# Sinkhorn-sorted attention and top-1 experts on one core: the units of attention in pairs, and the second half's sorting in a new order

## The chip, the cores and the metric

The kernel runs on one core of a Trainium2 chip. The metric is the device time of one execution in microseconds, the median of several; the kernel before took 172.33 us (three runs, 172.12 to 172.53).

The engines are named as in the rows of the profile: PE is TensorE (matmuls; PEld is its loading of weights), ACT is ScalarE, DVE is VectorE, POOL is GpSimd, SP is SyncE. Each works through its own list of instructions in order and waits for the others by semaphores. Matmul results land in PSUM, eight banks, from which ACT or DVE must fetch ("empty") them before the bank can be written again.

## The reference, cut to what matters

Four batches of eight heads, 768 rows in eight blocks of 96, 64 wide. A learned 8x8 matrix per head, made doubly stochastic in five rounds, mixes the blocks of K and of V; each block of Q attends to the mixed block of its number. The result, 3072 rows of 512, goes through eight experts of which each row uses the one with the largest gate:

```python
k_sorted = np.einsum('bhij,bhjcd->bhicd', P, k_b)          # mix the blocks of K, and of V
scores = scale * np.matmul(q_b, k_sb.transpose(0, 1, 2, 4, 3))
attn = np.exp(scores - max); attn = attn / (attn.sum() + 1e-09)
x = np.matmul(attn, v_sb)                                   # 3072 x 512 after the heads are joined
logits = x @ w_gate + modality_bias[modality_id]; e_idx = np.argmax(logits, axis=1)
out[mask] = gate_w[mask, None] * (np.maximum(x[mask] @ w1[e], 0.0) @ w2[e])   # for each expert e
```

The modality bias is so strong that all rows of one modality use one expert. The kernel counts on that (and has a slow path, not taken here): it has two experts, A and B, and sorts the rows by modality.

## The kernel before

**Attention.** The work is two halves of 16 units. Unit u takes four heads of two batches for one block: `scores` (eight small matmuls, tile `sc`), `expo` (one exponential of 96x768 on ACT into `attnT`), `av` (eight small matmuls, tile `op`; the 65th column is the sum of the weights), and on DVE a reciprocal (`rs_all`) and a multiplication into `xb`. Two units make one block of 96 rows for two batches. Before a half's units can run, V and K must be mixed: `sort_v` (eight chunks, tile `va`) and `sort_k` (six chunks, `ka`), and the queries turned, `prep_q` (tile `tq`). For the second half the V that was loaded into `v_in` is first copied in another order into `kv` by POOL (`relay_v`, four copies); K is then loaded into the place of V.

**Placement.** For each pair of units `place` multiplies `xb` by a permutation, so that rows of modality A stand from the left and rows of B from the right of `XT` (tile `pm`), and two casts of 72-wide windows bring them there at an offset that the engine first loads into a register (`load_offs`). `side` says which engine casts.

**Experts.** The rows are cut into 15 slots of 128 or 256 rows (the last of 224), each of A or of B, and each can start when so many blocks are placed. A slot has: `mG`, the gate's logits (tile `lg`) and their small steps on DVE and ACT; `mL1`, the first layer in two halves of 16 or 32 matmuls (tile `hp`), each half in two banks whose ReLU goes to `hT` by ACT or DVE; `mL2`, the second layer for 128 rows (tile `yp`), multiplied by the gate into `y` and scattered to the output by POOL. Which engine empties a bank was chosen by `pick`, from a running count of what each engine has been given.

**Order.** The program's order is each engine's order. `do_unit(u)` (from line 725) emits the scores of unit u+1, its exponential, one expert piece of the first list that can run (`run_pieces`), the output of unit u, and, where one is pending, a placement. So between two outputs there is always a unit's scores and one expert piece. In units 0 to 5 `av` also issues three or four matmuls of 252 columns into a spare part of its tile (line 474), whose results nobody reads; they are called fillers here. The tiles `sc`, `hp`, `op`, `pm` (of the blocks from 3 on), `va` and `ka` share three places of two banks each; `lg`, `tq`, `yp` (and `pm` before) share two places of one bank. A tile gets the place that was given up first, and its first matmul waits for the engine that empties the tile before it.

POOL also issues all large loads, in its order among its other work. After the units of the first half the kernel mixes V and K for the second with expert pieces between the chunks.

Of the kernel before, what the change touches and what calls it, by code (L numbers as in the profile page):

```python
# [24 lines left out]
def kernel(  # L25
# [442 lines left out]
    def av(u):  # L468
# [22 lines left out]
    def side(t, r):  # L491
        if t in (1, 7):
            return ("act", "dve")[r]
        return "act" if t % 2 == 0 or t == 5 else "dve"

    def load_offs(t):
        for o0, o1 in ([(0, 1), (1, 2)] if t in (1, 7) else [(0, 2)]):
# [54 lines left out]
    def mG(s):  # L552
# [11 lines left out]
        la, es, gt = la_all[:, ts], es_all[:, ts], gate[:, ts]  # L564
        nc.vector.tensor_tensor(la, lg[:, 0:nz, 0:E], bc_mid(st["bAB"][:, mi], nz), ALU.add)
        for z in range(nz):
# [3 lines left out]
            else:  # L570
                nc.vector.tensor_copy(dst, src)
        nc.scalar.activation(es, la, ACT.Exp)
# [5 lines left out]
    def relu(dst, src, n):  # L578
        if pick(n) == "act":
# [3 lines left out]
    def mL1(s, half):  # L583
# [4 lines left out]
        for b in range(2):  # L588
# [9 lines left out]
            ins = relu(hT[s % 2][:, half * 4 + b * nf // 2:half * 4 + (b + 1) * nf // 2, 0:n], hp[:, fs, 0:n], 512)  # L598
            tc.add_to_no_dep_group(grp, ins.ins)

    def mL2(s, z):
# [20 lines left out]
        else:  # L622
# [4 lines left out]
            if pick(512) == "act":  # L627
# [8 lines left out]

    pieces = []
    for s in range(NS):
        n = SLOTS[s][2]
        a = [(mG, (s,)), (mL1, (s, 0))]  # L640
        if s:
            a.append((mL2, (s - 1, 0)))
        if n > 128:
            a.append((mL1, (s, 1)))
        if s and SLOTS[s - 1][2] > 128:
            a.append((mL2, (s - 1, 1)))
        if s == 2:

            a = a[2:3] + a[:2] + a[3:]
        pieces += [(s, f, x) for f, x in a]  # L650
    pieces += [(NS - 1, mL2, (NS - 1, z)) for z in reversed(range(NZ[-1]))]
    pairs = [0]

    def can_run(piece):
        s, f, a = piece
        if f is mL2:
            return not any(p[1] is mL1 and p[2][0] == a[0] for p in pieces)
        return SLOTS[s][3] <= pairs[0] and not any(p[1] is mL2 and p[2][0] <= s - 2 for p in pieces)

    def run_pieces(n):  # L660
        ran = []
        while n:
            here = next((p for p in pieces if can_run(p)), None)
            if here is None:
                break
            pieces.remove(here)
            here[1](*here[2])
            ran.append(here)
            n -= 0 if here[1] is mG else 1
        return ran  # L670
# [45 lines left out]
    rank_off()  # L716
    for r in range(2):
        load_q(1, 0, r, 0)
    for z in range(2, 4):
        load_v(1, z)  # L720
    pending, ready = [], []

    def do_place():
        t = pending.pop(0)
        load_offs(t)
        place(t)
        ready.append(t + 1)

    def do_unit(u, last, n):
        if u < last:  # L730
            scores(u + 1)
            if u == 4:
                do_place()
            expo(u + 1)
            if u == 6:
                prep_q(0, 1, 2)
        if u == 13:

            for hq in range(2):
                prep_q(1, 0, hq, "dve")  # L740
        if 4 < u < 8:
            n = 0
        run_pieces(n)
        if ready:
            pairs[0] = ready.pop()
        av(u)
        if u in (4, 5, 7):
            prep_q(0, 1, u - 4)
        if u in (5, 7):
            run_pieces(1)  # L750
        if u % 2 == 0 and pending:
            do_place()
        if u % 2:
            pending.append(u // 2)

    for u in range(16):
        do_unit(u, 15 if u != 7 else 8, 2 if u == 12 else 1)
        if u == 8:
            make_bd(1)
        if u == 6:  # L760
            rank_p(1)
        for z in {9: (0, 1), 10: (2,), 11: (3,)}.get(u, ()):
            relay_v(z)
            if z:
                load_k(1, z - 1)
# [3 lines left out]
    for ch in range(8):  # L769
        sort_v(1, ch, ("act", "dve", "dve", "act")[ch] if ch < 4 else ("dve", "act")[ch % 2])  # L770
        if ch == 1:
            do_place()
        if ch in (1, 4):
            run_pieces(1)
        if ch == 3:
            pairs[0] = ready.pop()
    for ch in range(6):
        sort_k(1, ch, ("dve", "act")[ch % 2] if ch < 5 else "both")
        if ch in (1, 4):
            run_pieces(1)  # L780
    for hq in range(2, 4):
        prep_q(1, 0, hq)
    scores(16)
    expo(16)
    for u in range(16, 32):
        do_unit(u, 31, 1)
        if u in (16, 20):
            rank_p(u // 4 - 2)
        if 17 <= u < 21:
            prep_q(1, 1, u - 17)  # L790
    while ready or pending:
        run_pieces(1)
        if ready:
            pairs[0] = ready.pop()
# [229 lines left out]
```

## Time and profile before

| | |
|---|---|
| median of 3 runs | 172.33 us (172.12 to 172.53) |
| the profiled execution | 171.09 us |
| its span, first to last instruction | 169.4 us |
| PE busy | 150.5 us (89%) |
| DVE, ACT, POOL busy | 100.8 (60%), 94.9 (56%), 78.9 us (47%) |
| unit 0's output on PE | from 27.6 us of the span |
| unit 15's and unit 31's output | 65.7 and 127.8 us |
| last matmul | 164.2 us |

The profile shows one execution. Times in it are counted from the first instruction. The kernel has a start (to about 27 us: loads, the 8x8 matrices, mixing for the first half), the first 16 units (to 66), the mixing for the second half (to 83), the second 16 units (to 128) and experts alone (to 164); then the last rows are written. A busy PE is not PE at its peak, and ends of matmuls are modelled, so lengths of steps are best read from starts, or from the chain of waits.

### The profile page before, as it was taken

Reading aid. Unit: us, or ns where it says so; the run is one execution under the profiler, and the core shown is the slowest. Engines: PE = TensorE matmul, PEld = TensorE weight load, DVE = VectorE, ACT = ScalarE, POOL = GpSimd, SP = SyncE. Lnnn points to the kernel's source line nnn. Section 1 sums busy time; section 2 is a strip of 40 time slices with the busy share of each in tenths; the row PEclk is TensorE's granted clock in tenths of the full one; section 3 lists DMA queues with packets and bytes.
Section 4 is the critical chain, followed back from the end, with each engine's and each line's share of the span. In section 5 each row is a group of like instructions: output and inputs, shape, how many; then the busy total and the mean of one; then the engine's idle time right before and its main releaser. Section 6 shows DMA issues by size and latency. Waiting matters only on the chain.

```text
span 169.4 us, 5303 instructions
## 1 busy us (share of the span) xinstructions
PE 150.5 (89%) x2219; PEld 113.7 (67%) x2235; DVE 100.8 (60%) x261; ACT 94.9 (56%) x153; POOL 78.9 (47%) x150
## 2 busy tenths in 40 slices
PE   0489898899999999999899999999899999999970
PEld 0138886788667588777676768866677667776740
DVE  2778688578495387867675496674945613233430
ACT  4214767887557567665538757868466443432410
POOL 6888899778139997940204022020122222242432
PEclk9999999999999999999999999999999999999997
DMA  3999999999999988999101111001111111112221
GB/s 37 193 214 211 199 203 202 197 191 203 199 212 199 262 153 147 229 165 165 61 9 62 66 64 68 0 0 66 62 66 64 59 69 62 62 66 90 96 72 65
DMA packets 16303, 20.36 MB, mean 120 GB/s; under 512 B 9841, under 2 KB 11921, under 8 KB 16274
## 3 DMA queue, kind: packets, MB, share of 16 engines
q0 software_dynamic: 15648, 19.93, 60.5%
q8 instruction: 18, 0.29, 0.7%
q1 hardware_dynamic: 626, 0.05, 0.3%
q14 instruction: 11, 0.09, 0.2%
HBM read 27.31 MB, written 6.49 MB: 199 GB/s over the span
## 4 chain that ended last, share of the span: by engine, by line
PE 65%; POOL 9%; DVE 7%; issue 6%; ACT 6%; DMA 5%; POOLq 0%; ACTq 0%
PE hp L592 22%; PE yp L625 22%; DMA q_in<-in_q_dram 5%; PE sc L459 4%; PE op L479 4%; PE tq L334 3%; ACT XT L528 2%; PE pm L516 2%; POOL out_dram L631 2%; PE ka L324 2%; DVE xb L484 2%; PE va L311 2%; PE lg L560 2%; PE op L474 1%; POOL v_in L135 1%
## 5 line engine op out<-in xcount | busy, mean ns | idle before, releaser
L631 POOL DMA_INDIRECT out_dram<-y,ids x25 | 24.7, 989 | 77.8 <-ACT y L628 32.6
L625 PEld LDWEIGHTS <-hT 128*128 128x128 bf16 x192 | 17.6, 98 | 18.4
L465 ACT ACTIVATE attnT<-sc 96x768 bf16<-96x768 f32 x32 | 25.7, 807 | 6.7 <-PE sc L459 6.5
L580 ACT ACTIVATE hT<-hp 128x512 bf16<-128x512 f32 (+1 forms) x35 | 20.2, 588 | 11.6 <-PE hp L592 8.7
L592 PE MATMUL hp<-XT,wB 128*128 128x256 bf16 (+2 forms) x224 | 24.5, 263 | 0.2 <-DVE xb L484 0.2
L592 PE MATMUL hp<-XT,wA 128*128 128x128 bf16 (+1 forms) x256 | 23.1, 246 | 0.4 <-DVE xb L484 0.2
L484 DVE TENSOR_TENSOR xb<-op,rs_all 96x512 bf16<-96x512 f32 x32 | 22.0, 686 | 1.1
L625 PE MATMUL yp<-wA,hT 128*128 128x512 bf16 x88 | 21.5, 379 | 0.7 <-issue 0.5
L625 PE MATMUL yp<-wB,hT 128*128 128x512 bf16 x88 | 21.5, 379 | 0.6 <-issue 0.3
L592 PEld LDWEIGHTS <-wB 128*128 128x128 bf16 x224 | 19.8, 98 | 2.8 <-DVE xb L484 0.4
L628 ACT ACTIVATE y<-yp,gate 128x512 f32<-128x512 f32 x15 | 10.3, 688 | 19.1 <-PE yp L625 19.1
L592 PEld LDWEIGHTS <-wA 128*128 128x128 bf16 x256 | 19.3, 97 | 2.3 <-DVE xb L484 0.4
L528 ACT CAST XT<-pm 128x720 f32 x20 | 15.4, 768 | 4.5 <-PE pm L518 2.7
L581 DVE TENSOR_SCALAR hT<-hp 128x512 bf16<-128x512 f32 x15 | 10.3, 688 | 8.9 <-PE hp L592 8.8
L630 DVE TENSOR_SCALAR y<-yp,gate 128x512 f32<-128x512 f32 x9 | 6.8, 751 | 14.7 <-PE yp L625 14.7
L479 PEld LDWEIGHTS <-attnT 96*128 96x128 bf16 x256 | 11.8, 97 | 3.3
L483 DVE RECIPROCAL rs_all<-op 96x8 f32<-96x8 f32 x32 | 6.4, 199 | 11.7 <-PE op L479 11.6
L479 PE MATMUL op<-v_sb,attnT 96*128 96x65 bf16 x256 | 13.2, 193 | 0.0
L459 PE MATMUL sc<-qT,kT 64*128 64x96 bf16 x256 | 11.4, 205 | 1.9 <-DVE qT L102 0.7
L528 DVE CAST XT<-pm 128x720 f32 x12 | 10.9, 909 | 2.5 <-POOL pen L394 1.3
L147 POOL DMA_DIRECT2D q_in<-in_q_dram x16 | 12.3, 797 | 0.0
L100 ACT CAST v_sb<-va 96x1024 bf16<-96x1024 f32 x9 | 8.9, 1009 | 5.6 <-PE va L311 5.5
(166 smaller groups left out, 222.3 us busy)
## 6 DMA issues: line engine op xcount, KB each, us to landing
v_in<-in_v_dram POOLq DMA_DIRECT2D x8, 384.0 KB, 10.8
q_in<-in_q_dram POOLq DMA_DIRECT2D x16, 192.0 KB, 8.3
wA<-in_moe_w_dram POOLq DMA_DIRECT2D x4, 512.0 KB, 10.3
wB<-in_moe_w_dram POOLq DMA_DIRECT2D x4, 512.0 KB, 7.6
kv<-in_k_dram POOLq DMA_DIRECT2D x3, 512.0 KB, 10.8
v_in<-in_k_dram POOLq DMA_DIRECT2D x3, 512.0 KB, 6.2
out_dram<-y,ids POOLq DMA_INDIRECT x25, 2.8
modI<-in_moe_modality_id_dram SPq DMA_DIRECT2D x1, 24.0 KB, 4.4
```

The source lines that it names most:

```text
L147: nc.gpsimd.dma_start(out=q_in[r][z][:, 4 * hh:4 * hh + 4], in_=q[2 * g + r, 4 * hh:4 * hh + 4, z * 4 * BLK:(z + 1) * 4 * BLK] .rearrange( ...
L459: nc.tensor.matmul(sc[:, r, j * BLK:(j + 1) * BLK].rearrange("p (t r) -> p t r", t=3), kT[rows, x0:x0 + 128], qT5[rows, i // 4, h, :, i % ...
L465: nc.scalar.activation(attnT[u % 2][:, 0:8 * BLK].rearrange("p (r f) -> p r f", r=2), sc_tiles.pop(u)[0:BLK, :, 0:4 * BLK], ACT.Exp, scale ...
L479: nc.tensor.matmul(op[:, r, j * (D + 1):(j + 1) * (D + 1)], attnT[u % 2][:, c0:c0 + 128], v_sb[0:BLK, r * 64 + (hh * 4 + j) * 8 + i, 0:D + ...
L484: nc.vector.tensor_tensor(xb[t % XB][:, :, hh * 256:(hh + 1) * 256].rearrange("p r (j d) -> p r j d", j=4), o4[:, :, :, 0:D], rs_all[:, u] ...
L528: ins = (nc.scalar.copy if side(t, r) == "act" else nc.vector.tensor_copy)(d, s_).ins
L580: return nc.scalar.activation(dst, src, ACT.Relu)
L581: return nc.vector.tensor_scalar(dst, src, 0.0, None, ALU.max)
L592: mm = nc.tensor.matmul(hp[:, f, 0:n], w1_t[m][:, c, fc * 128:(fc + 1) * 128], XT[:, c, row:row + n], start=(c == 0), stop=(c == 3))
L625: nc.tensor.matmul(yp, hT[s % 2][:, f, hs], w2_t[m][:, f], start=(f == 0), stop=(f == 7))
L628: nc.scalar.activation(y, yp, ACT.Copy, scale=g_)
L631: ins = nc.gpsimd.indirect_dma_start(out=out, out_offset=bass.IndirectOffsetOnAxis(ap=ids[0:w, k_:k_ + 1], axis=0), in_=y[0:w], in_offset= ...
```

## The change

From unit 8 on the units are taken in pairs. A function `pair(t, one, two)` emits both units' scores and exponentials, then `one()`, then both outputs, then `two()`. In the plain case (`steady`) `one` holds the logits and a half of a first layer of a slot and the placement of the pair before, and `two` the rest of the gate's steps, at times a query transpose, and a second layer. The pieces of the experts are no longer found by a rule but written out by hand. In a pair the first bank of a half layer is emptied by DVE and the second by ACT (`DA`), second layers and query transposes by DVE, and all casts of placements by ACT but for one of block 1. The gate's exponential, sum and reciprocal (`gate_end`) come behind the outputs.

Units 0 to 7 keep their old order in the main, with these differences: units 4 and 5 have no fillers; the last transpose of the first half's queries stands ahead of unit 7's output instead of behind it; units 8 and 9 have their scores together, and the first layer of slot 1 behind them.

For the second half the two last loads of V stand ahead of two query loads; all four relay copies, the three loads of K and six query loads follow the scatter of slot 1 without a break, and the mixing has a new order of chunks and expert pieces. All four transposes of block 0 to 3's queries and one second layer more stand in it. Behind unit 31 the order of the experts is as before.

```diff
-        if u < 6:
+        if u < 4:
             for r in (0, 1, 0, 1)[:3 + (u > 2)]:
 ...
     def side(t, r):
-        if t in (1, 7):
-            return ("act", "dve")[r]
-        return "act" if t % 2 == 0 or t == 5 else "dve"
+        return "dve" if t == 1 and r else "act"
 ...
-    for r in range(2):
-        load_q(1, 0, r, 0)
     for z in range(2, 4):
         load_v(1, z)
+    for r in range(2):
+        load_q(1, 0, r, 0)
 ...
+    mG(0)
+    mL1(0, 0)
+    sc(7)
+    prep_q(0, 1, 2)
+    av(6)
+    put(2)
+    rank_p(1)
+    prep_q(0, 1, 3, "dve")
+    av(7)
+    DA = ("dve", "act")
+    def pair(t, one, two):
+        sc(2 * t, 2 * t + 1)
+        one()
+        av(2 * t)
+        av(2 * t + 1)
+        two()
+    def hidden(s, half):
+        if half == 0:
+            mG(s, late=True)
+        mL1(s, half, DA)
+    def steady(t, s, half, q_=None, l2=None):
+        def one():
+            hidden(s, half)
+            put(t - 1)
+        def two():
+            if half == 0:
+                gate_end(s)
+            if q_:
+                prep_q(*q_, "dve")
+            mL2(*l2, "dve")
+        pair(t, one, two)
+    steady(4, 1, 0, None, (0, 0))
+    make_bd(1)
+    steady(5, 2, 0, None, (1, 0))
+    for z in range(4):
+        relay_v(z)
+    for z in range(3):
+        load_k(1, z)
     for z, hh in ((0, 1), (1, 0), (1, 1)):
         for r in range(2):
             load_q(1, z, r, hh)
+    steady(6, 2, 1, None, (2, 0))
+    steady(7, 3, 0, None, (2, 1))
+    mL1(3, 1, DA)
+    put(7)
+    sort_v(1, 0, "act")
+    sort_v(1, 1, "dve")
+    mG(4)
+    mL1(4, 0, ("act", "act"))
+    sort_v(1, 2, "dve")
 ...
+    pair(8, lambda: hidden(5, 0), after_8)
+    steady(9, 6, 0, (1, 1, 1), (5, 0))
+    pair(10, before_10, after_10)
+    pair(11, before_11, lambda: mL2(7, 0, "dve"))
+    rank_p(3)
+    steady(12, 8, 0, None, (7, 1))
+    steady(13, 8, 1, None, (8, 0))
+    steady(14, 9, 0, None, (8, 1))
+    steady(15, 9, 1, None, (9, 0))
```

On POOL, before, from the last loads of V for the second half to the query loads (`kv` is written by the relay copies, `in_k_dram` is K, L631 is the scatter of a second layer's rows):

```order
L135 DMA v_in<-in_v_dram 128x1536 x2
L631 DMA out_dram<-y_86,ids 3072x512
L631 DMA out_dram<-y_87,ids 3072x512
L143 COPY kv<-v_in 128x64x24 x2
L139 DMA v_in<-in_k_dram 128x2048
L143 COPY kv<-v_in 128x64x24
L139 DMA v_in<-in_k_dram 128x2048
L143 COPY kv<-v_in 128x64x24
L139 DMA v_in<-in_k_dram 128x2048
L631 DMA out_dram<-y_88,ids 3072x512
L631 DMA out_dram<-y_89,ids 3072x512
```

The same place on POOL now (L635 is the scatter):

```order
L147 DMA q_in_74<-in_q_dram 128x4x192
L635 DMA out_dram<-y_86,ids 3072x512
L635 DMA out_dram<-y_87,ids 3072x512
L143 COPY kv<-v_in 128x64x24 x4
L139 DMA v_in<-in_k_dram 128x2048 x3
L147 DMA q_in_72<-in_q_dram 128x4x192
```

The K loads no longer stand between the copies but behind all four; the scatter ahead of the copies is still that of slot 1's rows (`y_87`), and the next scatters stand behind the query loads.

On ACT, before, around units 24 to 27 (`sc24` to `sc27` are the scores, `hp8` the first layer of slot 8, `pm10` and `pm12` placements, `y0` a second layer's result):

```order
L528 COPY XT_82<-pm10_2415 128x5x2x72
L465 ACTIVATE attnT0_77<-sc24_2428 96x768
L580 ACTIVATE hT1_85<-hp7_1_2438 128x512
L465 ACTIVATE attnT1_78<-sc25_2468 96x768
L572 ACTIVATE es_all_94<-la_all_93 128x16
L580 ACTIVATE hT0_84<-hp8_0_2495 128x512 x2
L465 ACTIVATE attnT0_77<-sc26_2543 96x768
L628 ACTIVATE y0_86<-yp7_0_2553,gate_95 128x512
L465 ACTIVATE attnT1_78<-sc27_2577 96x768
L580 ACTIVATE hT0_84<-hp8_1_2587 128x512 x2
```

The same units on ACT now, from the scores of unit 24 to the first layer beside units 26 and 27:

```order
L465 ACTIVATE attnT0_77<-sc24_2461 96x768
L465 ACTIVATE attnT1_78<-sc25_2470 96x768
L584 ACTIVATE hT0_84<-hp8_0_2495 128x512
L497 TENSOR_LOAD off_723
L526 ISA
L526 COPY XT_82<-pm11_2519 128x5x2x72
L526 ISA
L526 COPY XT_82<-pm11_2519 128x5x2x72
L576 ACTIVATE es_all_94<-la_all_93 128x16
L465 ACTIVATE attnT0_77<-sc26_2570 96x768
L465 ACTIVATE attnT1_78<-sc27_2579 96x768
L584 ACTIVATE hT0_84<-hp8_1_2590 128x512
```

The two exponentials of a pair stand together; one ReLU of the half layer follows instead of two or none, then the load of an offset and both casts of each placement, and the gate's exponential behind them; the second layers have left ACT.

## Rows read from the trace of the kernel before

**Rows 1.** Stretches: start:end, length, busy us (instructions) of PE PEld DVE ACT POOL, clock, DMA, GB/s

```profile
27.00:37.00 10.00, 9.33 (x181) 7.84 (x181) 7.07 (x21) 8.43 (x12) 7.78 (x26) 1.00 1.37 200
37.00:64.00 27.00, 25.75 (x396) 19.33 (x396) 17.27 (x48) 17.04 (x28) 19.08 (x17) 1.00 1.12 201
64.00:83.00 19.00, 18.20 (x378) 14.93 (x379) 13.90 (x21) 11.93 (x17) 9.52 (x12) 1.00 0.95 154
83.00:131.00 48.00, 45.93 (x669) 35.06 (x670) 30.87 (x79) 32.42 (x52) 8.33 (x9) 1.00 0.14 50
```

**Rows 2.** Chain of waits in order of time: start us, us, what

```profile
34.69 0.54 PE op L474 x4
...
41.17 1.80 PE hp L592 x32
...
65.89 0.24 PE op L479 x8
66.13 1.05 PE va L311 x16
...
77.98 1.64 PE ka L324 x96
...
84.20 0.21 PE lg L560 x5
...
88.81 0.46 PE tq L334 x12
...
106.64 0.24 PE op L479 x8
106.89 0.28 PE sc L459 x8
107.16 0.34 PE lg L560 x10
107.50 1.76 PE hp L592 x16
...
128.00 0.24 PE op L479 x8
...
148.55 1.73 PE yp L625 x8
```

**Rows 3.** Timeline of PE, a placement and what follows: start us, us, what

```profile
91.46 0.33 PE L516 MATMUL pm<-perm,xb 96*128 96x96 bf16 x4
...
91.98 0.53 PE L334 MATMUL tq<-ident,q_in 128*64 128x128 bf16 x12
```

**Rows 4.** Timeline of DVE and ACT near unit 4 and placement 2

```profile
34.97 0.69 DVE L484 TENSOR_TENSOR xb<-op,rs_all 96x512 bf16<-96x512 f32 x1
...
39.27 1.57 ACT L528 CAST XT<-pm 128x720 f32 x2
```

**Rows 5.** Page, costliest groups, the exponentials: busy us, mean ns; idle before

```profile
L465 ACT ACTIVATE attnT<-sc 96x768 bf16<-96x768 f32 x32 | 25.7, 807 | 6.7 <-PE sc L459 6.5
```

**Rows 6.** Timeline of PE and ACT behind a half layer

```profile
109.11 0.41 PE L479 MATMUL op<-v_sb,attnT 96*128 96x65 bf16 x8
...
109.31 0.60 ACT L580 ACTIVATE hT<-hp 128x512 bf16<-128x512 f32 x1 [0.28 <-PE hp L592]
```

**Rows 7.** Instructions of line 499, the offset loads on ACT: ns min/median/max

```profile
L499 ACTq TENSOR_LOAD <-off x11: 293/494/843, 29.6 to 125.7; - x11
```

**Rows 8.** Timeline of POOL, relays and a scatter, and ACT before it

```profile
51.70 5.67 POOL L143 COPY kv<-v_in 128x1536 bf16<-128x1536 bf16 x2
...
73.27 0.69 ACT L628 ACTIVATE y<-yp,gate 128x512 f32<-128x512 f32 x1 [1.53 <-PE yp L625]
...
74.23 1.04 POOL L631 DMA_INDIRECT out_dram<-y,ids  x1 [1.33 <-ACT y L628]
```

**Rows 9.** Page, DMA issues: KB each, median us from issue to landing

```profile
kv<-in_k_dram POOLq DMA_DIRECT2D x3, 512.0 KB, 10.8
v_in<-in_k_dram POOLq DMA_DIRECT2D x3, 512.0 KB, 6.2
```

More of the change, by code (lines that the diff above doesn't have):

```diff
@@ L491, in side @@
     def side(t, r):
-        if t in (1, 7):
-            return ("act", "dve")[r]
-        return "act" if t % 2 == 0 or t == 5 else "dve"
+        return "dve" if t == 1 and r else "act"
     def load_offs(t):
-        for o0, o1 in ([(0, 1), (1, 2)] if t in (1, 7) else [(0, 2)]):
+        for o0, o1 in ([(0, 1), (1, 2)] if t == 1 else [(0, 2)]):
             eng = ActEng if side(t, o0) == "act" else DveEng
@@ L550, in tiles, with mG @@
         return [(row, w0)] + [(row + w0 + 128 * z, 128) for z in range((n - w0) // 128)]
-    def mG(s):
+    def mG(s, late=False):
         m, row, n = slot(s)
@@ L563, in mG @@
         ts = slice(TOFF[s], TOFF[s] + nz)
[L564 removed]
+        la = la_all[:, ts]
         nc.vector.tensor_tensor(la, lg[:, 0:nz, 0:E], bc_mid(st["bAB"][:, mi], nz), ALU.add)
@@ L571, in mG, with gate_end @@
                 nc.vector.tensor_copy(dst, src)
+        if not late:
+            gate_end(s)
+    def gate_end(s):
+        ts = slice(TOFF[s], TOFF[s] + NZ[s])
+        la, es, gt = la_all[:, ts], es_all[:, ts], gate[:, ts]
         nc.scalar.activation(es, la, ACT.Exp)
@@ L635, in mL2 @@
         tc.add_to_no_dep_group("out", ins.ins)
[L637 to L670, printed above, removed]
     rank_b()
@@ L716, with sc, put @@
     rank_off()
+    for z in range(2, 4):
+        load_v(1, z)
     for r in range(2):
         load_q(1, 0, r, 0)
[L719 to L724, printed above, removed]
+    def sc(*us):
+        for u in us:
+            scores(u)
+        for u in us:
+            expo(u)
+    def put(t):
         load_offs(t)
         place(t)
[L727 to L765, printed above, removed]
+    sc(1)
+    av(0)
+    sc(2)
+    av(1)
+    sc(3)
+    av(2)
+    put(0)
+    sc(4)
+    av(3)
+    scores(5)
+    put(1)
+    expo(5)
+    av(4)
+    prep_q(0, 1, 0)
+    sc(6)
+    av(5)
@@ L768, with after_8, before_10, after_10 @@
             load_q(1, z, r, hh)
[L769 to L794, printed above, removed]
-        if pending:
-            do_place()
+    steady(6, 2, 1, None, (2, 0))
[7 more added lines that the diff above has]
+    sort_v(1, 2, "dve")
+    sort_v(1, 3, "act")
+    sort_v(1, 4, "dve")
+    mL2(3, 0, "dve")
+    sort_v(1, 5, "act")
+    sort_v(1, 6, "dve")
+    sort_v(1, 7, "act")
+    sort_k(1, 0, "dve")
+    sort_k(1, 1, "act")
+    mL1(4, 1, DA)
+    sort_k(1, 2, "dve")
+    prep_q(1, 0, 0, "act")
+    mL2(3, 1, "dve")
+    sort_k(1, 3, "act")
+    sort_k(1, 4, "dve")
+    prep_q(1, 0, 1, "act")
+    prep_q(1, 0, 2, "dve")
+    sort_k(1, 5, "act")
+    prep_q(1, 0, 3, "dve")
+    mL2(4, 0, "dve")
+    def after_8():
+        gate_end(5)
+        rank_p(2)
+        prep_q(1, 1, 0, "dve")
+        mL2(4, 1, "dve")
+    def before_10():
+        put(9)
+        mL2(6, 0, "dve")
+    def after_10():
+        prep_q(1, 1, 2, "dve")
+        mG(7)
+        mL1(7, 0, DA)
+    def before_11():
+        prep_q(1, 1, 3, "dve")
+        hidden(7, 1)
+        put(10)
+    pair(8, lambda: hidden(5, 0), after_8)
[7 more added lines that the diff above has]
+    steady(15, 9, 1, None, (9, 0))
+    mG(10)
+    mL1(10, 0)
+    put(15)
+    mL2(9, 1)
+    mL1(10, 1)
     cm = small("cm", 4)
@@ L823 @@
     last = NS - 1
-    while pieces:
-        for here in run_pieces(1):
-            if here[0] == last and here[1] is mG:
-                flag_b()
-            if here[0] == last and here[1] is mL1 and here[2][1] == 1:
+    for s in range(11, NS):
+        mG(s)
+        if s == last:
+            flag_b()
+        mL1(s, 0)
+        mL2(s - 1, 0)
+        if SLOTS[s][2] > 128:
+            mL1(s, 1)
+            if s == last:
                 flag_c()
+        if SLOTS[s - 1][2] > 128:
+            mL2(s - 1, 1)
+    mL2(last, 1)
+    mL2(last, 0)
     order.close()
```

14 lines of the change are left out of this document (8 added, 6 removed).

## The prediction

> **What bounds the kernel now.** I first read the stretches of the span with the busy time of each engine. TensorE (PE in the rows) is busy 9.33 of 10.00 us, 25.75 of 27.00, 18.20 of 19.00 and 45.93 of 48.00, and its granted clock is 1.00 in all of them [rows 1]. No other engine comes near that (ScalarE's 8.43 of the first 10 is the most), so PE's own order sets the time, and what a new order of the same matmuls can give back is PE's idle time: 0.67 + 1.25 + 0.80 + 2.07 = 4.8 us from 27 to 131. Behind 131 the kernel runs experts alone, in the same order before and after but for which engine empties a bank.
>
> Next I read the chain of waits in order of time: here one row is the length of one step on PE, and the reader is to take the unit prices from it [rows 2]: an output (op, 8 matmuls) 0.24, scores of a unit (sc) 0.28, the gate's logits (lg, 10) 0.34, half of a first layer (hp, 16) 1.76, one second layer (yp) 1.73, a query transpose (tq) 0.46, a chunk of sorted V (va) 1.05 / 2 = 0.53, a chunk of sorted K (ka) 1.64 / 3 = 0.55. A placement (pm, ten matmuls) is not whole in one row; from its start at 91.46 to the next step at 91.98 it takes 0.52 [rows 3]. Check: from the output of unit 23 at 106.64 to that of unit 31 at 128.00 stand 8 op, 8 sc, 2 lg, 4 hp, 4 pm and 4 yp, 1.92 + 2.24 + 0.68 + 7.04 + 2.08 + 6.92 = 20.88 by the prices and 21.36 in the rows: waits make up 0.48, 0.06 a unit.
>
> With them I lay the new order out on PE from a point where both orders have done the same work, and compare at four such points. "Behind" is the new kernel's time less the old one's at the same work done.
>
> **Start of the pairs, units 4 to 9.** Two units lose their fillers, four matmuls each: 2 x 0.54 = 1.08 us of PE [rows 2]. Little of it arrives. The first half layer of slot 0 writes a bank that the output of unit 4 had, and VectorE empties that at 34.97 + 0.69 = 35.66 [rows 4]. The end of the last filler, 34.69 + 0.54, is followed by output, transpose and logits, 0.24 + 0.46 + about 0.2, and so by the half layer at some 36.1; it moves by 0.3 to 0.4 (I take 0.3), and the rest turns into a wait. What follows is new. The last transpose of the first half of the queries now stands ahead of unit 7's output. It needs a bank that the first cast of placement 2 frees. The two casts took 1.57 from 39.27 [rows 4]; moved by 0.3 the first ends at 39.8. Transpose 0.46, output 0.24 plus 0.1 for a switch to other weights, scores of unit 8 0.28: 40.9. The half layer of slot 1 needs the exponential of unit 8 (its bank), 0.81 on ScalarE [rows 5]: it starts at 40.9 + 0.15 + 0.81 = about 41.9. Unit 9's scores wait in this time for the copy of that transpose, behind a 768-wide compare on VectorE, and cost nothing more. The half layer ends at 43.7. Before, it ran 1.80 from 41.17, and unit 9's scores followed: 43.25 [rows 2]. Behind by 0.45.
>
> **A pair in the steady state.** scores 2 x 0.28, logits 0.34, half layer 1.76, placement 0.52, outputs 2 x 0.24, second layer 1.73: 5.39 us with logits, 5.05 without. The added wait is at the second output: its bank is that of the half layer, whose second half ScalarE empties. In a row of before that step started 0.20 after the matmuls had ended (109.31, the next output at 109.11) and took 0.60 [rows 6]: 0.80, against placement and first output, 0.76. With a release this is about 0.1 us of wait in each of ten pairs; 5.5 and 5.15. Queued behind it on PE are a second layer and the next scores; all wait with it. If the wait were nothing I would win 1.0 in ten pairs, and if ScalarE came late by a whole exponential I would lose 8. I take 0.1 since nothing else is queued on ScalarE then: its two exponentials have ended some 0.5 us before. The casts are now all on ScalarE, and each needs its offset read first, 0.29 to 0.84 us [rows 7]; 0.80 + 0.3 + 1.57 = 2.7 after the half layer they end, and the next unit that needs their bank comes 0.52 + 0.48 + 0.1 + 1.73 + 0.28 = 3.1 after it. So they stay hidden, by 0.4.
>
> Pairs 4 to 7: from 43.7, rest of pair 4 (placement, outputs, wait, second layer) 2.85, then some 0.3 for the small matmul of make_bd and for logits that now need the bank of the second layer just before them, 5.5, 5.15, 5.5: 63.0. Before: unit 15's output ends at 65.89 + 0.24 = 66.13, with a half layer (1.76) and two transposes (0.92) more done: 63.45 [rows 2]. Behind by -0.45, so this stage gives 0.9.
>
> **Sorting of the second half.** Half layer 1.76, placement 0.52: PE is at the first chunk of V at 65.3. That chunk needs all four relay copies on GpSimd. Before, they began at 51.70, and two took 5.67 [rows 8]; now all four stand behind the scatter of slot 1. Its second layer ends at 43.7 + 2.85 + 0.3 + 5.5 = 52.35, and VectorE empties it behind two outputs and a gate, by about 53.3. A scatter starts 0.3 after its y (73.27 + 0.69 to 74.23) and takes 1.0 [rows 8], then 2 x 5.67: 65.9. So PE waits 0.6 where it did not before. Then 8 chunks of V 4.2, logits 0.34, two half layers 3.52, three second layers 5.19, 6 chunks of K 3.3, four transposes 1.84, two scores 0.56 = 18.95, and some 0.5 of short waits where a chunk's bank is not yet empty: 85.4. Before: the logits of slot 5 start at 84.20 with one second layer less done, 85.93 [rows 2]. Behind by -0.5.
>
> **Pairs 8 to 15.** Pair 8 has no placement: 0.2 + 1.80 + 0.48 + 0.1 + 0.46 + 1.73 = 4.8. Pairs 9, 10 and 11 by the same prices, with a transpose each: 5.85, 5.95, 5.6. That is 107.6. Before: the output of unit 23 ends at 106.88, one score more and one second layer less: 108.33 [rows 2]. Behind by -0.7, so 0.2 is won. Pairs 12 to 15: 2 x 5.5 + 2 x 5.15 = 21.3; before, 106.64 to 128.00, 21.36 [rows 2]. Nothing.
>
> **Tail.** The same steps on PE; VectorE takes most of the emptying in slots 10 and 11 at first, in about three quarters of PE's time. Nothing.
>
> **Sum.** +0.45 - 0.9 - 0.05 - 0.2 + 0 = -0.7 us. My lay-out has only the waits that I looked for, while the old kernel's times have all of theirs: PE idles 2.07 us in its 16 units from 83 to 131, 0.13 a unit [rows 1], of which I gave the new ones 0.05. The difference on 24 units is 1.9 that may be missing at most; I put a quarter, 0.5, in, since the check above left 0.06 a unit. So -0.2 us on the profiled execution (171.09: span 169.4 and 1.7 around it). That execution lies 1.24 below the median of the runs, 172.33; I carry the difference over: 172.1. A measurement of this kernel can tell 0.2%, 0.34 us, from no change; so the forecast is no change to speak of, with an own range of 171.1 to 173.1.
>
> Of the clock the rows say that it stays at the full level, 2.4 GHz, through stretches in which PE idles 4 to 7% [rows 1]; the new waits are under 1 us each, so the sum has no term for it. The Trainium skill, "TensorE: Matmul & The Clock Gate", section "What's actually happening", speaks against the change here: the array gets only half of its clock after it was idle, and the full one after it was busy again, and the fillers that go are work for just that. By that rule the result could be the fourth rival.
>
> **Rivals.**
> First, faster: the two junctions are covered. If the first half layer of slot 1 does not wait for unit 8, and the relays end before PE comes (their scatter 0.6 us sooner), 0.45 + 0.6 = 1.05 is not paid: 171.0. For it: VectorE and ScalarE are busy 63 to 84% of the stretches that hold them [rows 1], so either may be free earlier than I have it. Against it: both waits are for single named instructions, not for a queue.
>
> Second, slower: the K loads come late. They were issued one by one between relays and landed after 6.2 us in the median; now three are issued in a row at 65.9 with six query loads behind them. The three of the first half, issued in a row at the start, took 10.8 [rows 9]. PE needs the first at about 65.9 + 8.4 (8 chunks 4.2, logits 0.34, half layer 1.76, second layer 1.73, waits 0.4) = 74.3, that is 8.4 after the issue. Up to there it is free; at 10.8 it costs 2.4, 174.5. Against it: the loads at the start had four V loads ahead of them, and here the queue is empty.
>
> Third, the pairs do not change what is waited for: PE is never idle for what pairs remove, gains and losses are all under 0.1 us: 172.3.
>
> Fourth, the clock falls to 1.2 GHz after the wait at the sort. Were it there for one pair's length of work, the 5.4 us of that would be paid twice: 177.5. No row shows a granted clock under 1.00 before 131.
>
> **How the numbers follow.** Forecast 0.50, faster 0.22, slower 0.22, third 0.05, clock 0.01. The forecast's own spread (1.0 us either side of -0.2) has 0.43 of it more than 0.34 us below the old time, 0.32 within that and 0.25 above: faster 0.21 + 0.22 = 0.43; same 0.16 + 0.05 = 0.21; slower 0.13 + 0.22 + 0.01 = 0.36. The range reaches down to 170.4 (the faster rival, and half of the ten waits of 0.1 gone) and up to 174.2 (nearly the slower one's middle); beyond lie the late loads' upper end, the clock, and a gain above 1.9 us.
>
> **What would show it.** Right: in the new trace PE idles less from 44 to 63; a wait of some 0.6 us stands ahead of the first chunk of V and is ended by GpSimd's relay copy; the second output of a pair stands about 0.1 us late behind ScalarE's hT; the last output lies within 1 us of 128. Wrong: K chunks that wait for a DMA; scores that wait for casts of a placement; an idle time of PE from 84 to 130 well under 1 us or above 3; a granted clock under 1 before the tail.

## The result: slower by 0.7%, and the profile after

The changed kernel takes 173.53 us in the median of 7 runs (172.60 to 174.15), the kernel before 172.21 beside it; the ratio is 1.0071 (95%: 1.0050 to 1.0093). Run once more in the last series it came out at 1.0110 (1.0091 to 1.0128). The forecast was no change to speak of, 172.1.

The profiled execution is the shortest of the seven, 172.6 with a span of 171.0, against 171.09 and 169.4 before: 1.6 more. By stretches (columns as in [rows 1]):

```profile
27.00:37.00 10.00, 8.91 (x182) 7.55 (x182) 7.25 (x22) 8.81 (x13) 7.80 (x26) 1.00 1.37 199
37.00:64.00 27.00, 25.64 (x384) 19.05 (x382) 18.34 (x49) 17.89 (x28) 16.76 (x15) 1.00 0.97 177
64.00:83.00 19.00, 17.32 (x347) 13.81 (x346) 11.19 (x16) 11.28 (x15) 11.34 (x14) 1.00 1.06 177
83.00:131.00 48.00, 45.59 (x682) 32.84 (x676) 31.69 (x80) 28.87 (x44) 8.68 (x9) 1.00 0.15 56
```

PE is idle 1.68 from 64 to 83 (0.80 before) and 2.41 from 83 to 131 (2.07), at a granted clock of 1.00 throughout. The reader is to see that the two bad stretches are those of the sorting and of pairs 8 to 15, not the one of the first pairs.

The chain of waits in order of time (start, us, what) shows the sorting stage, where [rows 2] had whole chunks in a row:

```profile
62.91 2.79 POOL kv L143
65.70 0.04 issue
65.74 1.07 PE va L311 x16
...
74.81 0.45 issue
75.27 0.28 PE ka L324 x6
...
81.46 0.75 DVE y L634
82.21 0.04 issue
82.25 0.53 PE tq L334 x12
82.78 0.33 PE ka L324 x13
83.11 0.67 issue
83.79 0.47 PE ka L324 x19
```

Four things stand ahead of PE here: the relay copy, which takes 2.79 (two took 5.67 in [rows 8]; PE idle 0.67 at 65.74), a stop inside a K chunk for which the profile shows no releaser (0.45), a transpose that waits for a second layer's evacuation (0.36 of PE), and a second stop inside a K chunk, after 13 of its 32 matmuls (0.67).

The same view for pairs 8 to 11:

```profile
91.24 0.94 DVE perm L420
92.17 0.48 DVE qT L102
92.65 0.04 issue
92.69 0.27 PE lg L558 x5
...
101.02 0.75 DVE y L634
...
103.44 0.46 DVE qT L102
...
104.64 0.60 DVE hT L585
105.28 0.04 issue
105.32 0.61 ACT hT L584
105.93 0.04 issue
105.97 1.91 PE hp L596 x16
```

Twice the chain runs through VectorE. The logits of slot 6 start 0.46 late, since their bank's transpose is copied behind a compare of 0.94. The second half layer of slot 7 starts 1.03 late: VectorE does an evacuation, two outputs, a copy and a gate from 101.02 on before it empties the first bank, and ScalarE's part of the same half layer waits for VectorE's.

And a pair that goes as laid out, pair 12:

```profile
110.69 0.45 PE sc L459 x16
111.14 0.34 PE lg L558 x10
111.48 1.76 PE hp L596 x16
...
113.67 0.24 PE op L479 x8
113.93 0.40 PE op L479 x8
114.33 1.73 PE yp L629 x8
116.06 0.45 PE sc L459 x16
```

From scores to scores 5.37; the second output stands 0.40 where an output takes 0.24, so 0.16 for ScalarE's half of the half layer, whose length was read from [rows 6].

At the four points of the prediction and at the end of pair 15 the new kernel is behind, at equal work, by +0.16 (placement at 43.41 for 43.25), -0.71 (62.74 for 63.45), +1.00 (86.93 for 85.93), +2.29 (110.62 for 108.33) and +1.68 (131.49 for 129.81). It had 0.24 less on the clock when the first changed instruction came (unit 5's scores at 31.35 for 31.59).

| stage | forecast | measured |
|---|---|---|
| start of the pairs | +0.45 | +0.40 |
| pairs 4 to 7 | -0.9 | -0.87 |
| sorting | -0.05 | +1.71 |
| pairs 8 to 11 | -0.2 | +1.29 |
| pairs 12 to 15 | 0 | -0.61 |
| tail | 0 | 0 |

### The profile page after: what moved, and what is told of

Same layout as the page of the kernel before. It is cut to its first block, busy times and chain, and to the rows that moved or that the text cites. A ratio compares the mean times of both kernels' runs of the same rounds, so it can differ in the third digit from the quotient of the medians.

```text
span 171.0 us, 5301 instructions
## 1 busy us (share of the span) xinstructions
PE 150.8 (88%) x2227; PEld 111.7 (65%) x2227; DVE 105.6 (62%) x273; ACT 89.2 (52%) x140; POOL 78.7 (46%) x150
## 3 DMA queue, kind: packets, MB, share of 16 engines
HBM read 27.31 MB, written 6.49 MB: 198 GB/s over the span
## 4 chain that ended last, share of the span: by engine, by line
PE 51%; POOL 18%; issue 11%; DVE 8%; DMA 5%; ACT 4%; POOLq 1%; ACTq 0%
PE hp L596 17%; PE yp L629 14%; POOL kv L143 7%; DMA q_in<-in_q_dram 5%; POOL out_dram L635 5%; PE op L479 4%; PE tq L334 3%; PE sc L459 3%; PE va L311 3%; PE ka L324 2%; DVE xb L484 2%; DVE y L634 2%; PE pm L514 2%; ACT XT L526 2%; PE lg L558 1%
## 5 line engine op out<-in xcount | busy, mean ns | idle before, releaser
L635 POOL DMA_INDIRECT out_dram<-y,ids x25 | 25.1, 1002 | 80.2 <-DVE y L634 43.3
L465 ACT ACTIVATE attnT<-sc 96x768 bf16<-96x768 f32 x32 | 24.5, 803 | 10.8 <-PE sc L459 10.8
L526 ACT CAST XT<-pm 128x720 f32 x31 | 23.9, 771 | 4.7 <-PE pm L516 1.7
L585 DVE TENSOR_SCALAR hT<-hp 128x512 bf16<-128x512 f32 (+1 forms) x26 | 17.6, 683 | 11.4 <-PE hp L596 11.0
L584 ACT ACTIVATE hT<-hp 128x512 bf16<-128x512 f32 (+1 forms) x24 | 14.2, 592 | 17.1 <-PE hp L596 15.1
L629 PE MATMUL yp<-wA,hT 128*128 128x512 bf16 x96 | 22.7, 379 | 0.0
L634 DVE TENSOR_SCALAR y<-yp,gate 128x512 f32<-128x512 f32 x20 | 15.0, 748 | 11.4 <-PE yp L629 11.3
L479 PEld LDWEIGHTS <-attnT 96*128 96x128 bf16 x256 | 10.2, 97 | 1.8 <-issue 0.2
L143 POOL COPY kv<-v_in 128x1536 bf16<-128x1536 bf16 x4 | 11.2, 2850 | 0.0
L102 DVE CAST v_sb<-va 96x1024 bf16<-96x1024 f32 x7 | 8.5, 1219 | 4.3 <-PE va L311 4.2
L576 ACT ACTIVATE es_all<-la_all 128x16 f32<-128x16 f32 (+1 forms) x15 | 3.2, 211 | 13.9 <-DVE la_all L563 13.9
```

The source lines that it names most:

```text
L143: nc.gpsimd.tensor_copy(kv[:, 0:BLK * D].rearrange("p (d c) -> p d c", c=BLK)[:, :, cs], v_in[:, cs].rearrange("p c d -> p d c"))
L465: nc.scalar.activation(attnT[u % 2][:, 0:8 * BLK].rearrange("p (r f) -> p r f", r=2), sc_tiles.pop(u)[0:BLK, :, 0:4 * BLK], ACT.Exp, scale ...
L479: nc.tensor.matmul(op[:, r, j * (D + 1):(j + 1) * (D + 1)], attnT[u % 2][:, c0:c0 + 128], v_sb[0:BLK, r * 64 + (hh * 4 + j) * 8 + i, 0:D + ...
L526: ins = (nc.scalar.copy if side(t, r) == "act" else nc.vector.tensor_copy)(d, s_).ins
L629: nc.tensor.matmul(yp, hT[s % 2][:, f, hs], w2_t[m][:, f], start=(f == 0), stop=(f == 7))
L634: nc.vector.tensor_scalar(y, yp, g_, None, ALU.mult)
```

## The experiments

Each is an edit of the changed kernel, unless said, shown with its loops written short; ratios are to the kernel before, run beside it. The changed kernel itself stands at 1.0071 and 1.0110. These two differ by 0.4% for one and the same kernel, so what a single edit is worth is read from its trace, and the ratio only bears it out.

**Relays between the loads (e1).**

```
+    relay_v(0), relay_v(1)                  # ahead of steady(5): slot 1's scatter comes behind
     steady(5, 2, 0, None, (1, 0))
-    for z in range(4): relay_v(z)
-    for z in range(3): load_k(1, z)
+    load_k(1, 0); relay_v(2); load_k(1, 1); relay_v(3); load_k(1, 2)
```

> Two relay copies move ahead of the scatter of slot 1 (GpSimd is free from 49.3), the three K loads stand between the later relays as in the kernel before, then the six query loads. Main theory: the changed kernel loses in the sorting stage by the relay wait (0.67) and by gaps inside K chunks (0.45 + 0.67) that come from the nine loads landing in one burst at 72 to 82. Here the first V chunk does not wait and the loads end some 4 us earlier, so both go at least in part: 0.7 to 1.8 us shorter than the changed kernel, 171.7 to 172.8. Rival (the gaps belong to the order of PE's own instructions, not to the loads): 0.67 less and the gaps stay at the same chunks, 172.9. Second rival (PE only waits later, for K): no gain, 173.5.

0.9972 (0.9960 to 0.9983). Both stops are gone, but the relay wait is still there, 0.61: the first relay had to wait for its V load until 51.82, and the scatter stood in the middle. So the gain is that of the K chunks and what queued behind them: from the first V chunk to the scores of unit 16 the stage took 18.76 for 20.74. The edit moves relays and K loads at once, so it does not say which of the two counts.

**Four query loads later (e2).**

```
-    for z, hh in ((0, 1), (1, 0), (1, 1)): load_q(1, z, r, hh)
+    load_q(1, 0, r, 1)                      # r in 0, 1; the other four behind sort_k(1, 2)
```

> Four of the six query loads (those of the last quarter of the queries) move 14 us later in GpSimd's queue; nothing else changes. Burst theory: the second gap in a K chunk (0.67) and the wait of 0.36 at a query transpose behind it go, the first gap (0.45, among the K loads) stays or shrinks: 0.6 to 1.0 us shorter than the changed kernel, 172.5 to 172.9; a new gap may show at 84 to 88 where the loads now land. Rival (the gaps follow PE's instructions): no change, both gaps stay. Second rival: the first transpose of pair 8 waits for its query load, up to 1 us longer.

1.0069 (1.0054 to 1.0084): nothing won. The stop is longer, after the same 13 matmuls. Its PE timeline (start, us, engine, line, what; in brackets the idle time ahead):

```profile
82.52 0.40 PE L324 MATMUL ka<-bd,v_in 64*64 64x64 bf16 x13
84.26 0.47 PE L324 MATMUL ka<-bd,v_in 64*64 64x64 bf16 x19 [1.34 <-issue]
```

This run does not test the burst. GpSimd runs ahead of PE in its list, so the four loads were not issued 14 us later but 6 to 7 (the third to sixth query load stand between 68.8 and 71.9 in the changed kernel):

```profile
75.04 1.62 POOL L147 DMA_DIRECT2D q_in<-in_q_dram  x2
```

They were under way when PE stopped: the DMA share is 1.52 from 80 to 81 and 1.63 from 81 to 82.

**The four query loads left out (e5).** Those units compute with the first half's queries.

```
-    for z, hh in ((0, 1), (1, 0), (1, 1)): load_q(1, z, r, hh)
+    load_q(1, 0, r, 1)
```

> The changed kernel without the four query loads of its last quarter (those units then use the first half's queries); every other instruction stands as it was. In four profiles the last K chunk stops after 13 matmuls, 0.67 to 1.34 us, at the same instruction, and PE goes on 1.1 to 1.45 us after a 16 KB packet of the instruction queue has been moved (81.3 to 82.6 in the changed kernel); with the relays between the loads that packet came at 79.3, the loads had ended, and there was no stop. Theory (PE's next instructions come late because loads hold the DMA engines): without the 0.77 MB that end at 83, the packet comes before 80 and the stop goes; with it the wait of 0.36 behind it may go: 0.7 to 1.1 us shorter than the changed kernel. Rival (it is the place in the program alone): the stop stays, 0.7 or more, no change.

The theory's number failed: the stop stays, 0.62. That does not clear the loads: those that are left run to about 80 (DMA share 0.99 from 79.0 to 79.5, 0.63 and 0.21 in the next two half microseconds), and the packet of the expectation comes at 80.17, when they let up. All work ends 1.47 earlier than in the changed kernel's profile (the last scatter starts at 165.32 for 166.79), and yet it takes 175.19 (1.0235; 1.0212 to 1.0259): 8.2 us of its span lie behind the start of that scatter, for 4.2 in the changed kernel, and no row of the engines stands there. What they are stays open; the runs don't tell.

**Fillers back in units 4 and 5 (e6).**

```
-        if u < 4:
+        if u < 6:
```

> The changed kernel with the four filler matmuls back in units 4 and 5 (2 x 0.54 us of PE). The prediction had 0.3 to 0.4 of these 1.08 arrive, the rest lying under waits for casts. In the changed kernel three waits for casts and outputs follow (0.45, 0.40, 0.18) up to the placement at 43.41. Theory: that placement starts 0.2 to 0.5 later, 0.2 to 0.5 longer in all. Rival (PE had the time to spare only by 0.45): 1.0 later.

1.0048 (1.0022 to 1.0073), so by the ratio the fillers cost nothing that can be seen. The half layer of slot 1 starts at 41.86 for 41.63: 0.23 later, as expected. This run told more than it was meant to. It has 8 matmuls more ahead of the K chunks, and the stop moved by 8:

```profile
82.67 0.63 PE L324 MATMUL ka<-bd,v_in 64*64 64x64 bf16 x27 [0.70 <-issue]
```

27 matmuls are left of the chunk instead of 19. The stop stands at a count of PE's instructions, not at a tile.

**Slot 7's gate late and its first half layer on ScalarE (e3), and each alone (e10, e11).**

```
-        mG(7); mL1(7, 0, DA)
+        mG(7, late=True); mL1(7, 0, ("act", "act"))     # e10: late alone; e11: ("act", "act") alone
...
         hidden(7, 1)
+        gate_end(7)                                      # not in e11
```

> In pair 10 and 11 slot 7's gate ends after its second half layer, and ScalarE empties both banks of its first half layer. Theory: the 1.03 wait ahead of that second half layer is VectorE's queue (a second layer's evacuation, two outputs, a transpose copy and a gate from 101.0 to 104.6 ahead of the first bank, and ScalarE's part waits for VectorE's). With both on ScalarE they end at 104.6 and the wait is under 0.15: 0.9 us shorter than the changed kernel, 172.6. Rival (it is the exponential of the gate that holds ScalarE): only what the gate took, 0.4, is won. Second rival: the exponentials of pair 11, now behind two ReLUs, end late and the pair's first output waits: no gain.

> Of the edit at slot 7 only the late gate: VectorE still empties the first bank and ScalarE the second behind it. If VectorE's queue is what the second half layer of slot 7 waits for (evacuation, two outputs, a copy, then the bank), the wait falls from 1.03 by what the gate took there, 0.4 to 0.5, to some 0.55. If the exponential on ScalarE were the cause, it would go altogether.

> Of the edit at slot 7 only the engine: ScalarE empties both banks, the gate stays ahead of them, so its exponential (ready when VectorE's sum is, 103.99) stands in front of both. If VectorE's queue is the cause, the wait falls from 1.03 to some 0.45, by 0.6; both parts are then needed for the 1.0 that the whole edit took away. If the gate's exponential were nothing, it would fall to 0.1.

e3: 0.9996 (0.9974 to 1.0017). The half layer follows the transpose at once:

```profile
103.21 0.53 PE L334 MATMUL tq<-ident,q_in 128*64 128x128 bf16 x12
103.67 1.92 PE L596 MATMUL hp<-XT,wA 128*128 128x256 bf16 x16
```

From the scores of unit 22 to those of unit 24 it takes 5.57 for 6.66. In e10 and then e11, which ran once each, so that only their traces count, the wait is 0.52 and 0.33:

```profile
105.62 1.91 PE L596 MATMUL hp<-XT,wA 128*128 128x256 bf16 x16 [0.52 <-ACT hT L584]
...
105.83 1.91 PE L596 MATMUL hp<-XT,wA 128*128 128x256 bf16 x16 [0.33 <-ACT hT L584]
```

Neither part does it alone, and with the gate away half of the wait is left: VectorE's queue is the cause, and the gate is a part of it. (In e11, with both banks on ScalarE, what is left is the gate's exponential ahead of them, which waits 2.48 for VectorE's sum.)

**The compare later (e4).**

```
-        rank_p(2); prep_q(1, 1, 0, "dve"); mL2(4, 1, "dve")
+        prep_q(1, 1, 0, "dve"); mL2(4, 1, "dve"); rank_p(2)
```

> VectorE's 0.94 us compare for the permutations of blocks 16 to 23 moves behind a transpose copy and a second layer's evacuation in pair 8. Theory: the logits of slot 6 (0.46 wait for that copy's bank) start at once: 0.45 us shorter than the changed kernel, 173.1. Rival: the wait moves to the half layer of slot 6 or to the placement, whose permutations are ready later: no change, 173.5.

1.0021 (1.0001 to 1.0040). The logits follow the scores without a wait, and pair 9 takes 5.84 from scores to scores for 6.49.

**Offsets read early (e7).**

```
     def pair(t, one, two):
+        load_offs(t - 1)              # t != 8; put(t - 1) becomes place(t - 1)
         sc(2 * t, 2 * t + 1)
```

> In the pairs ScalarE reads the two offsets of a placement ahead of the pair's exponentials instead of behind its ReLU. In two of five profiles of this family one such read took up to 1.73 us in pair 6, the casts behind it ended late, and the next scores (0.48 to 0.65) and a half layer (0.55 to 0.73) waited for them; in the changed kernel's own profile the longest was 0.88 and nothing waited. Theory: no wait for a cast in the pairs; 0 to 0.6 shorter than the changed kernel, by the share of runs that have a long read. Rival: a long read now holds the exponentials, and the first output of a pair waits instead: no change or longer.

1.0032 (1.0015 to 1.0048), no wait for a cast in the pairs, and a longest read of 1.39 that held nothing. That such a read costs when it stands ahead of the casts is seen in the second profile of the changed kernel (f1), whose longest read is 1.76 for 0.84 in [rows 7]; first the reads (min/median/max ns), then the scores of unit 15:

```profile
L497 ACTq TENSOR_LOAD <-off x16: 290/516/1764, 29.8 to 132.8; - x16
```

```profile
58.72 0.35 PE L459 MATMUL sc<-qT,kT 64*128 64x96 bf16 x8 [0.52 <-ACT XT L526]
```

**Three mends together (e8, again as f2).** All relays, K and query loads stand ahead of slot 1's scatter, relay and K load in turn; with them the edits e3 and e4.

```
+    for z in range(4):
+        relay_v(z)
+        if z: load_k(1, z - 1)
+    for z, hh in ((0, 1), (1, 0), (1, 1)): load_q(1, z, r, hh)
     steady(5, 2, 0, None, (1, 0))
```

> Together: all four relay copies with the K loads between them and the query loads, ahead of slot 1's scatter; slot 7's gate late and its first half layer emptied by ScalarE; the compare for the permutations behind the evacuation in pair 8. The single edits gave 1.7, 1.3 and 0.9 against the changed kernel by their ratios. Theory (each removes a wait of its own; the relay wait of 0.6, which stayed in the first of them, goes too, since the scatter of 1.0 is out of the way): 3.3 to 4 us shorter than the changed kernel, a ratio to the kernel before of 0.984 to 0.988. Rival (the gains share the loads' gaps, which vary from run to run, and overlap): 2.0 to 2.5 shorter, 0.993 to 0.996.

> The changed kernel once more, on one chip with the three kernels of this series. If the stops inside K chunks ahead of the block edge (75.27 in its first profile) and the lower clock of two other profiles belong to a chip, both show in all four kernels or in none; if to a kernel, in some. By the singles: 1.005 to 1.007 of the kernel before.

> The three mends once more (0.990 before, on another chip than the changed kernel's first run). If its gain is its own: 1.5 to 1.9% under the changed kernel beside it, so 0.988 to 0.992 of the kernel before. If it was the chip's: within 0.7% of the changed kernel.

0.9901 (0.9867 to 0.9934), and 0.9893 (0.9873 to 0.9912) beside the changed kernel's 1.0110: 169.31 for 172.89 us. It beats both kernels, by 1.1% and 2.1%. In f2 PE idles 0.10 of the 48 us from 83 to 131:

```profile
83.00:131.00 48.00, 47.90 (x686) 34.61 (x685) 32.70 (x85) 29.54 (x47) 9.66 (x9) 1.00 0.14 51
```

The traces of f1 and f2 differ by 0.44 before the first edit can act, and by 4.03 at unit 24's scores. Of the 3.6 between, 0.69 lies ahead of the first K chunk, 1.30 from there to the scores of unit 16, 0.51 in pair 9, 1.09 in pair 11 (the distances of the same scores and chunks in the two traces). The 0.69 belongs to no mend: it stands whole at the scores of unit 15, behind f1's long read (above), which f2 does not have (longest 0.77). The relay wait is gone and has won nothing by itself: slot 4's half layer started at 66.98 in the changed kernel; in e8 it starts at 67.08, after a wait for the cast of placement 7 that the relay wait had covered:

```profile
67.08 1.91 PE L596 MATMUL hp<-XT,wB 128*128 128x256 bf16 x16 [0.77 <-ACT XT L526]
```

**Split casts (e9, f3), with early offsets (e12), and with fillers (f4), each on top of the three mends.**

```
-        return "dve" if t == 1 and r else "act"
+        return "dve" if t in (1, 7) and r else "act"     # f4: u < 6 in its place; e12: with load_offs of e7
...
-        for o0, o1 in ([(0, 1), (1, 2)] if t == 1 else [(0, 2)]):
+        for o0, o1 in ([(0, 1), (1, 2)] if t in (1, 7) else [(0, 2)]):
```

> The three mends together, and the two casts of placement 7 stand on ScalarE and VectorE side by side, as in the kernel before, instead of one after the other on ScalarE. With the relays early the first V chunk waits for nothing (65.01), but slot 4's half layer two steps later starts at 67.08, after 0.77 of waiting for the second cast (its bank); in the changed kernel it started at 67.05 behind the relay wait. Theory (the relay wait only covered that of the cast, which is why taking it away gave nothing): with both casts side by side the half layer starts 0.5 to 0.7 earlier and the kernel is as much shorter than with the three mends, 0.986 to 0.988 of the kernel before. Rival: the next V chunk's bank then waits for VectorE's casts, no gain.

> The kernel with the three mends and the split casts, and the offsets read ahead of the exponentials in the pairs (that alone gave 0.6 by its ratio). Theory: the offset reads are off the way of the casts: 0.2 to 0.6 shorter again, 0.983 to 0.987 of the kernel before. Rival: the reads never held anything but in runs with a long one: the same as the kernel with the split casts within 0.2%.

> The three mends with the split casts once more. It came out 1.3% above the three mends, on another chip, with a profile in which the clock was at half for 3.4 us. If split casts cost that (the next bank waits for ScalarE's copy, 0.70 for 0.77, which says nothing is won or lost): the same as the three mends within 0.3%. If they do cost: 1% above.

> The three mends with the four fillers back in units 4 and 5, which cost 0.25 us at the first placement in the single test. If PE's waits of 0.45 and 0.40 there are what lets the clock fall at 41.7 in some executions (1.7 us each), this kernel shows none of the two-valued times that the kernel with split casts showed, and is 0.25 above the three mends at most, or below. If the clock falls whatever stands there: two-valued times, and 0.25 above.

Beside each other, f3 is at 0.9890 (0.9870 to 0.9909) and f4 at 0.9901 (0.9883 to 0.9918), both level with f2: the split casts win nothing, since the same half layer now waits 0.68 for the V chunk's copy on ScalarE, and the fillers cost under 0.1. e9 and e12 came out at 1.0043 (1.0019 to 1.0067) and 1.0005 (0.9977 to 1.0033) in a series in which the kernel before takes 172.4 instead of 171.2 (the record has both series under chip 2); f3 is the same kernel as e9, so most of that loss is not the order's. In the profile of e9 the clock was granted at 1.2 GHz for a while, here the stretch and in it a half layer of 3.56 us for 1.95:

```profile
37.00:64.00 27.00, 25.25 (x366) 19.36 (x368) 16.79 (x45) 17.63 (x27) 17.96 (x16) 0.94 1.10 191
```

```profile
41.65 3.56 PE L596 MATMUL hp<-XT,wA 128*128 128x128 bf16 x32 [0.18 <-ACT attnT L465]
```

The profile of e12 shows it too, in the sorting. PE stops three times inside the first K chunk, for 0.48, 0.47 and 0.52 between 74.2 and 76.1; the clock falls right behind, and a half layer takes 3.14 for 1.92:

```profile
75.41 0.19 PE L324 MATMUL ka<-bd,v_in 64*64 64x64 bf16 x1 [0.47 <-issue]
76.12 1.03 PE L324 MATMUL ka<-bd,v_in 64*64 64x64 bf16 x31 [0.52 <-issue]
77.08 3.14 PE L596 MATMUL hp<-XT,wB 128*128 128x256 bf16 x16
```

```profile
77.00:78.00 1.00, 1.00 (x11) 0.69 (x7) 0.61 (x1) 0.81 (x1) 0.00 (x0) 0.50 1.04 404
```

f4 does not tell whether the fillers guard against the fall at 41.7, as no profile of that series shows it.

## Why the prediction was wrong, step by step

- **The unit prices and the start: right.** Start +0.40 for +0.45. Pairs 8 and 10 took 4.79 and 5.75 (4.8 and 5.85 by the prices; the prediction has the prices of pairs 9 and 10 the other way round). The fillers were 1.08 of PE and 0.23 of time (e6); the prediction had 0.3.
- **Pairs 4 to 7: right**, -0.87 for -0.9. Pairs 12 to 15 take 5.37, 5.12, 5.36 and 5.02 where 5.5 and 5.15 were laid out: 0.43 of the -0.61. The rest is on the other side: between the points used here the old kernel took 21.48, and 21.3 was set against 21.36 as nothing.
- **The relay wait: right in place and size (0.67 for 0.6), wrong as a cost.** In f1 PE comes later, and it is under 0.2. Where it went (e8), a cast on ScalarE held the same half layer to 67.08. The casts were priced as hidden by 0.4, for the scores alone; the half layer of slot 4 was not looked at. The faster rival, which lived on this 0.6, falls too.
- **The failing term is the allowance for unseen waits: 0.5, with 1.9 as its upper end.** The lay-out without it came to -0.7, and the profile to +1.68 at the end of pair 15: 2.4 was missing. Five single waits that the lay-out lacked come to 0.45 + 0.67 + 0.36 + 0.46 + 1.03 = 2.97, less 0.5 of short waits that the sorting stage was already given. The allowance was carried over from the old order's idle time per unit. That says nothing of a new order: the waits are not spread, they are five.
  Two of them (0.46 ahead of slot 6's logits, 1.03 ahead of slot 7's second half layer) are in f1 too, at the same size, and could have been had by laying out VectorE's queue in pairs 8 to 11 as PE's was: pair 9 took 6.49 for 5.95 and pair 11 6.66 for 5.6, and with the edits of e4 and e3 they are 0.51 and 1.09 shorter (f2 beside f1). The stop in the last K chunk (0.67; 1.18 in f1) has no row of its kind in [rows 1] to [rows 9]. The other two (0.45, 0.36) are not in f1 at all; there a cast behind a long read costs 0.52 at unit 15's scores and 0.59 at slot 4's half layer instead, and the sum at unit 24 is the same within 0.2 (110.83 for 110.62). With the mends the forecast for the end of pair 11, 107.6, is bettered: unit 24's scores start at 106.94.
- **The slower rival named the right place, but the wrong mechanism.** It wanted K chunks that wait for a DMA, for 2.4. No chunk of the changed kernel waits for a load; PE stops inside the last one, 0.57 to 1.34 in ten profiles with the late loads, and not in the five of e1, e8, f2, f3 and f4, where relays and loads start sooner. The other two with early loads, e9 and e12, have a stop of 0.20 and 0.19 there, after 10 matmuls, and longer ones in the first chunk.
- **The clock rival** did not happen: 1.00 up to the tail in both profiles of the changed kernel. Two of the 17 profiles of the new order show that it can: e9 in the first half, at an estimated 1.6 us (mean clock 0.94 over 27 us), and e12 at the sort, where the rival had it, at an estimated 1.7 (0.91 over 19) for the rival's 5.4. The Trainium skill's rule in "TensorE: Matmul & The Clock Gate", section "What's actually happening" (half of the clock after the array was idle), agrees with e12 in kind only: PE stood still just before, for 1.47 us in all, but in three stops with matmuls between them. It does not tell e9 from f3: before 41.65 PE had waited 0.40, 0.16 and 0.18 within 2.1 us, and f3, the same kernel with the same three waits, stays at 1.00.
- **The signs:** PE's idle time from 44 to 63 fell (0.53 for 0.87), and the second output late by 0.1 (0.16) and the relay wait came. The last output, due within 1 us of 128, starts at 129.5 and so gave the warning. PE's idle time from 84 to 130 (1.73) stayed inside the band given, so that sign was too wide to warn. Scores that wait for a cast, a sign of being wrong, stand in f1 and not in the first profile.
- **A slip in the chances:** an even spread of 1.0 us either side of -0.2 gives 0.43, 0.34 and 0.23 where 0.43, 0.32 and 0.25 stand; nothing hangs on it.

## What to carry to other kernels

Lay out the queue of every engine that empties banks, not only that of the bound engine: 1.49 of the 2.97 us were VectorE's order of small instructions, each harmless alone. A wait that is seen is a cost only if nothing stands behind it; ask what the same step would wait for next. Where a tight loop of small matmuls follows a burst of loads, look for stops that no semaphore explains. And profile the same kernel twice before each wait gets its price: of five waits here two came back at their size, one at another size, and two not at all.

## What the runs showed that was not expected

**PE seems to run out of instructions.** The stop in the last K chunk stands at one count of PE's instructions and moved by 8 matmuls when 8 were added (e6). The profile has a queue of instructions, q8, with 18 packets of 0.29 MB in all, one for some 130 matmuls, so it is taken here to carry PE's code; the packet that belongs to the stop, in the DMA view of 81 to 82 of the changed kernel and of 79 to 80 of e1 (packets, MB, share):

```profile
q8 instruction: 1, 0.02, 7.8%
```

```profile
q8 instruction: 1, 0.02, 6.1%
```

In narrower stretches it begins at 81.32 and takes 1.25; PE goes on at 83.79, 1.2 after its end (1.1 to 1.45 in all ten profiles with the stop). In e1 it begins at 79.32 and PE, there at about 81.95, does not stop. Stretches cut at the packets' starts between 90 and 118 hold 133, 130 and 129 matmuls. The Trainium skill, "Runtime: NRT & Kernel Launch", section "Instruction fetch mechanics", says that code comes in 16 KiB blocks of 256 instructions and that a block's edge is mostly hidden: the size agrees (0.29 MB in 18; about 128 matmuls with their weight loads), the hiding does not hold here. What makes the packet late is not shown. That loads hold it up was argued only: it comes early when the loads were issued early (before, 79.20; e1; e8, 78.36), in e5 it comes at 80.17, as the loads that are left let up, and in the changed kernel at 81.32, as the DMA share falls from 1.6 to 1.0; but in e2 it comes at 81.83 with the share still at 1.6. e1, with PE's own order unchanged, shows that this count alone does not make the stop; relays and loads were moved together there, and no run parts them.

**A register read of an offset** takes 0.3 to 1.9 us on ScalarE (the 1.9 in e2) in the same kernel family; in [rows 7] it was 0.29 to 0.84. Every read over 0.9, in ten of the 17 profiles of the new order, is one that starts between 54.7 and 56.1, in pair 6; elsewhere none takes more than 0.89. Its cause is open, as is that of the stop at 74.81, which e9, e10 and e12 show in other places and f1, the same kernel, does not.
